# A half store and a weight fetch queued behind the first stacks of the fourth segment

## The chip, the core and the metric

The kernel runs on one core of a Trainium2 chip. The metric is device time of the whole program in microseconds (us), the median of several executions. Engine names are those of the profile: PE is the matmul engine (PEld its weight load), DVE the vector engine, ACT the scalar engine, POOL the GpSimd engine, and SP the sync engine, which here issues every DMA of the kernel, in one order, and computes nothing.

## What is computed

An adaLN block over 2048 tokens of width 1024: layernorm with a modulation, segmented attention with a compressive memory, a residual, a second modulated layernorm, and a token-mixing MLP. The attention is where the change lies. Cut to that:

```python
h = _layernorm(x) * (1 + ca) + sa
for s in range(4):                                  # segments of 512 tokens, 32 heads of 32
    qs, ks, vs = q[:, :, s], k[:, :, s], v[:, :, s] # h @ wq, h @ wk, h @ wv
    a_dot = softmax(qs @ ks.T * scale + mask) @ vs
    num, den = phi(qs) @ M, phi(qs) @ z + 1e-6
    o = g * num / den + (1.0 - g) * a_dot
    M, z = M + phi(ks).T @ vs, z + phi(ks).sum()
x = x + ga * (o @ wo)                               # then x + gb * mixer(layernorm(x) ...)
```

## The kernel before

Single-precision products are made of three reduced-precision ones: each operand is split into a high part (`hi`, an ACT copy, line 119) and the rest (`lo`, a DVE subtraction, line 122), so that a tile "has arrived" for PE in two steps.

**Order of the attention.** The heads are taken in 8 groups of four, the segments in two passes of two. An iteration `t` is one group in one segment of the pass: `t` = 0, 1 are group 0 in segments 0 and 1, `t` = 2, 3 are group 1 in the same two, `t` = 4, 5 group 2. What the title calls the fourth segment is the fourth iteration, `t` = 3. Each iteration has these steps, which the builder lays out over later and later slots, so that three iterations are in flight at a time:

- `project(t)`: matmuls of the group's k and v columns (`nps`, line 192; `kv_chunk`) and q columns (`qps`, line 200), then the split of k and q into a tile `sg`.
- `stack(t, h)` (lines 368 to 376): three DMAs of 128 KB, lines 374, 375 and 376, that lay the hi and lo parts of one head's q and k on top of each other in a tile `sk`. Line 374 takes the hi parts, 375 q's hi and k's lo, 376 q's lo and k's hi. There are two sets of four `sk` tiles, used by even and odd `t`.
- `maxima(t, h)` (line 478): three sorts of matmul, `sx`, `sy` and `sz`, out of the stack, and DVE's masked maxima of them (line 480); after two heads a transpose `nmps` (line 486) and the small stores of its result into `sk` (line 493).
- `scores(t, h)` (lines 515, 518 and 522, tiles `a`), exponentials on ACT into `p`, their split into `ph` (ACT, line 529) and the rest (POOL, line 531); `values(t, h)` (line 549, `pv`), whose normalisation on DVE is lines 552, 554 and 556.
- `memory(t)`: read-out `rd` (line 450) and update `up` (line 460).

Beside this run chores from a table `todo`, by slot number. Two matter here. `fetch_part` (line 150) loads half of a group's weights, 512 KB, into a tile tagged `raw` (three buffers), and `split_part` splits it later; `keep_w` (line 173) stores the split weights in DRAM for the second pass. `token_tile(tt)` (lines 252 to 272) prepares 128 tokens of the second pass's segments: it normalises the 512 KB tile `gaw`, and stores its hi part (`hix`, also a `raw` tile) and its lo part (in place in `gaw`) to DRAM, 512 KB each (line 271). Afterwards `load_gaw` (line 671) loads the next 128 tokens into the same `gaw`, which a DVE `BN_STATS` (line 127) reads first.

**Who sets the order.** A list scheduler orders each engine's instructions at build time by its own estimate of times. `tc.issue_after(x)` tells it to place what follows behind instruction `x`. On the chip each engine runs its list in that order, and so does SP with the DMAs.

Of the kernel before, what the change touches and what calls it, by code (L numbers as in the profile page):

```python
# [41 lines left out]
def attention_and_mlp(ctx, tc, x, wq, wkv, wo, beta, w1, b1, w2, b2, c, wm_a, wm_b, out):  # L42
    nc = tc.nc
    V, A, G, T, SY = nc.vector, nc.scalar, nc.gpsimd, nc.tensor, nc.sync
# [27 lines left out]
    def bank(tag, bufs, name):  # L72
        return psum.tile([P, 512], F32, tag=tag, bufs=bufs, name=name)
# [73 lines left out]

    def fetch_part(g, kind, part):
        r = a.tile([P, D], F32, tag="raw", bufs=3, name=f"raw{kind}{g}_{part}")
        SY.dma_start(r, (wkv if kind == "v" else wq)[g, :, 1024 * part:1024 * part + 1024])  # L150
        return r

    def split_part(g, kind, part, r):

        for i in range(2):
            w = aw.tile([P, 2, 512], F32R, tag="w", bufs=8, name=f"w{kind}0_{g}_{part}_{i}")
            split(w, r[:, 512 * i:512 * i + 512], A, V)
            W[0, g][kind, 2 * part + i] = w

    def load_part(g, pr, kind, part, res):  # L160

        if pr == 0:
            split_part(g, kind, part, fetch_part(g, kind, part))
            return
        for i in range(2):
            w = aw.tile([P, 2, 512], F32R, tag="w", bufs=8, name=f"w{kind}{pr}_{g}_{part}_{i}")
            SY.dma_start(w.bitcast(F32), wsp[g, 2 * part + i if kind == "v" else 4 + i])
            res[kind, 2 * part + i] = w

    def keep_w(g):  # L170
        for kind, n in (("v", 4), ("q", 2)):
            for i in range(n):
                SY.dma_start(wsp[g, i if kind == "v" else 4 + i], W[0, g][kind, i].bitcast(F32))
# [62 lines left out]
    def norm_x(pool, t):  # L236
        mv = ln_stats(pool, t, "a")
        V.tensor_scalar(mv[:, 3:4], mv[:, 0:1], -1.0, mv[:, 2:3], op0=ALU.mult, op1=ALU.mult)
        A.activation(t, t, AF.Identity, scale=mv[:, 2:3], bias=mv[:, 3:4])
# [12 lines left out]
    def token_tile(tt):  # L252

        r = gaw
        norm_x(a, r)
        for half in range(2):
            ps = bank("s2", 2, f"hpl{tt}_{half}")
            for i in range(4):
                ct = 4 * half + i
                T.transpose(ps[:, 128 * i:128 * i + 128], r[:, P * ct:P * ct + P], ident)  # L260
            for i in range(4):
                ct = 4 * half + i
                A.activation(r[:, P * ct:P * ct + P], ps[:, 128 * i:128 * i + 128], AF.Identity,
                             scale=saca[:, ct, 1:2], bias=saca[:, ct, 0:1])
        hi = a.tile([P, D], F32, tag="raw", bufs=3, name=f"hix{tt}")
        A.copy(hi.bitcast(F32R), r)
        for c in (slice(0, 512), slice(512, 1024)):
            G.tensor_tensor(r[:, c].bitcast(F32R), r[:, c], hi[:, c], op=ALU.subtract)
        i = tt % 4
        for part, t in enumerate((hi, r)):  # L270
            SY.dma_start(hT1[tt // 4 - 2, :, :, part, P * i:P * i + P].rearrange("k p n -> p k n"),
                         t.rearrange("p (k n) -> p k n", k=NK))

    right = tc.tile_pool(name="st2", bufs=1, side="right")
    s2p = right.__enter__()
# [90 lines left out]
    last_sk, last_nt = {}, {}  # L366
# [226 lines left out]
    todo = {}  # L593

    def plan(n, f, engines=""):
        todo.setdefault(n, []).append((f, engines))
# [21 lines left out]
    with tc.issue_after(normed_v.ins):  # L618
# [4 lines left out]
        with tc.issue_after(h_a.ins), tc.issue_after(h_v.ins):  # L623
            project(0, 2)
            project(0, 3)
    parts = (("v", 0), ("v", 1), ("q", 0))
    raw_1 = [fetch_part(1, *part) for part in parts]
    seg_chunks(1, 2, 8)
    project(1, 0)
# [33 lines left out]
    def later(n, fetch, m, f, engines):  # L663

        got = []
        plan(n, lambda: got.append(fetch()))
        plan(m, lambda: f(got[0]), engines)
# [5 lines left out]
    for i in range(8):  # L673
        later(6 * i, lambda i=i: load_gaw(i),
              6 * i + 3, lambda r, i=i: token_tile(8 + i), "V")
    for g in range(2, NG):
        n = 8 * g - 13
        plan(n, lambda g=g: W.__setitem__((0, g), {}))
        for kind, part, n0, n1 in (("v", 0, 0, 1), ("v", 1, 1, 3), ("q", 0, 2, 4)):
            later(n + n0, lambda g=g, kind=kind, part=part: fetch_part(g, kind, part),  # L680
                  n + n1, lambda r, g=g, kind=kind, part=part: split_part(g, kind, part, r), "A")
        plan(n + 4, lambda g=g: keep_w(g))
# [8 lines left out]
    for n in range(-LEADS, 4 * NI + VL):  # L691
# [5 lines left out]
        if 0 <= m + 4 < 4 * NI:  # L697
            t = (m + 4) // 4
# [448 lines left out]
```

## Time and profile before

| | us |
|---|---|
| median of 3 runs | 2222.85 (2221.31 to 2225.35) |
| the profiled execution | 2224.45 |
| its span, first to last instruction | 2222.7 |
| what lies around the span | 1.75 |
| mean granted PE clock | 0.997 |
| PE, DVE, ACT and POOL busy | 98%, 75%, 51%, 33% of the span |

In a timeline each row has a start, a length, the engine, the line of the kernel, the operation, out<-in by the program's names without numbers, and in brackets the idle time of the engine ahead of it and what ended it. "issue" there means that the profile shows nothing that the engine waited for; a DMA's landing can stand behind it. A row with a count merges equal instructions. Rows marked SPq are DMAs at their issue on SP. In a table of stretches the number in brackets counts instructions; PEclk is the granted clock, and the DMA share can be over 1 because packets overlap.

### The profile page before, as it was taken

What the parts mean: (1) busy time and instruction counts of PE and PEld (TensorE: products, weight loads), DVE (VectorE), ACT (ScalarE), POOL (GpSimd) and SP (SyncE); (2) the same over time, 40 slices, a digit from 0 to 9 for tenths busy, and PEclk for the clock granted to TensorE, in tenths of its full rate; (3) what the DMA queues carried; (4) which work ended last, traced back from release to release, by engine and by line L of the source; (5) the groups of instructions that cost most, each with busy time, mean ns of one, the idle gap of its engine ahead of it and who ended that gap; (6) DMA issues with size and microseconds to landing.
All of it is one profiled execution on the core that took longest, in us unless ns stands there. A gap on an engine that the chain in (4) does not pass through costs nothing.

```text
span 2222.7 us, 38130 instructions
## 1 busy us (share of the span) xinstructions
PE 2184.5 (98%) x13786; PEld 1881.3 (85%) x13786; DVE 1673.2 (75%) x3762; ACT 1132.7 (51%) x2050; POOL 723.6 (33%) x831
## 2 busy tenths in 40 slices
PE   8999999999999999999999999999999999999999
PEld 5988998889999999888888888888888888888887
DVE  7677777767777677664858766888888887869687
ACT  5476777755666666654636533533334242424232
POOL 2165766656767677553002200033330000000000
PEclk9999999999999999999999999999999999999999
DMA  7656665587566665664754686655556541414134
GB/s 287 193 172 195 183 185 160 169 297 246 167 195 203 199 206 176 192 227 133 232 204 185 227 318 255 246 225 207 214 203 222 199 153 60 142 57 147 57 124 152
DMA packets 175184, 423.05 MB, mean 190 GB/s; under 512 B 17524, under 2 KB 71828, under 8 KB 166036
## 3 DMA queue, kind: packets, MB, share of 16 engines
q1 hardware_dynamic: 174996, 420.61, 57.4%
q8 instruction: 110, 1.80, 0.3%
q14 instruction: 78, 0.64, 0.1%
HBM read 244.62 MB, written 125.06 MB: 166 GB/s over the span
## 4 chain that ended last, share of the span: by engine, by line
PE 82%; DVE 6%; DMA 5%; ACT 3%; issue 1%; POOL 1%; SPq 1%; DVEq 0%; ACTq 0%
PE mx L927 47%; PE nps L192 10%; PE qps L200 7%; PE po L797 6%; PE pv L549 3%; DMA otr<-oT 1%; PE a L515 1%; DMA sk<-sg 1%; PE sz L478 1%; PE sx L478 1%; POOL p L531 1%; PE a L522 1%; PE sy L478 1%; PE a L518 1%; PE up L460 1%
## 5 line engine op out<-in xcount | busy, mean ns | idle before, releaser
L927 PE MATMUL mx<-bU,sp 128*128 128x512 f32 x2352 | 534.7, 389 | 1.0 <-DVE ac L934 0.9
L927 PEld LDWEIGHTS mx<-bU,sp 128*128 128x128 f32 x2352 | 441.1, 188 | 94.1 <-issue 1.3
L119 ACT CAST sp<-wr 128x384 fp32r<-128x384 f32 (+2 forms) x408 | 217.2, 545 | 433.0 <-PE mx L927 354.8
L192 PE MATMUL nps<-wv,h 128*128 128x256 f32 x3072 | 430.9, 283 | 1.1 <-DVE h L122 0.7
L927 PE MATMUL mx<-bA,sp 128*128 128x512 f32 x1764 | 430.5, 389 | 0.0
L531 POOL TENSOR_TENSOR p<-p,ph 128x640 f16<-128x640 f32 x256 | 377.7, 1476 | 121.7 <-ACT ph L529 116.8
L192 PEld LDWEIGHTS nps<-wv,h 128*128 128x128 f32 x3072 | 402.7, 190 | 8.8 <-DVE h L122 1.8
L927 PEld LDWEIGHTS mx<-bA,sp 128*128 128x128 f32 x1764 | 331.2, 188 | 68.7
L122 DVE TENSOR_TENSOR sp<-wr,sp 128x384 fp32r<-128x384 f32 (+2 forms) x408 | 259.1, 646 | 28.9 <-ACT sp L119 28.7
L934 DVE TENSOR_TENSOR ac<-mx,ac 128x512 f32<-128x512 f32 x280 | 189.4, 685 | 85.1 <-PE mx L927 84.5
L200 PE MATMUL qps<-h,wq 128*128 128x512 f32 x768 | 196.4, 399 | 0.0
L529 ACT CAST ph<-p 128x1280 f16<-128x1280 f32 x128 | 161.1, 1258 | 49.7 <-POOL p L527 49.2
L797 PE MATMUL po<-wo,ots 128*128 128x512 f32 x768 | 179.7, 391 | 1.4 <-ACT ots L119 1.4
L527 POOL TENSOR_SCALAR_AFFINE_SELECT p<-p 128x256 f32<-128x256 f32 x256 | 135.5, 535 | 119.9 <-ACT p L524 70.4
L797 PEld LDWEIGHTS po<-wo,ots 128*128 128x128 f32 x768 | 143.4, 188 | 31.2 <-ACT ots L119 1.8
L927 PE MATMUL mx<-bB,sp 128*128 128x512 f32 x588 | 164.0, 389 | 0.0
L200 PEld LDWEIGHTS qps<-h,wq 128*128 128x128 f32 x768 | 140.5, 189 | 27.1
L927 PEld LDWEIGHTS mx<-bB,sp 128*128 128x128 f32 x588 | 110.4, 188 | 22.9
L934 DVE TENSOR_TENSOR cc<-mx,cc 128x512 f32<-128x512 f32 x140 | 94.9, 684 | 41.7 <-PE mx L927 41.6
L480 DVE CUSTOM_DVE_ANT_0 sz<-sz,mask 128x512 f32<-128x512 f32 x128 | 89.2, 697 | 47.8 <-PE sz L478 46.9
L480 DVE CUSTOM_DVE_ANT_0 sx<-sx,mask 128x128 f32<-128x128 f32 (+1 forms) x256 | 93.3, 365 | 35.2 <-PE sx L478 31.5
L516 ACT ACTIVATE p<-a,shift 128x512 f32<-128x512 f32 x128 | 88.0, 688 | 43.6 <-PE a L515 39.6
(207 smaller groups left out, 3193.9 us busy)
## 6 DMA issues: line engine op xcount, KB each, us to landing
sk<-sg SPq DMA_DIRECT2D x384, 128.0 KB
wr<-in_w_dram SPq DMA_DIRECT2D x28, 1024.0 KB
wr<-in_w_dram SPq DMA_DIRECT2D x32, 768.0 KB
bstu<-ucd SPq DMA_DIRECT2D x28, 768.0 KB
wsp<-wv SPq DMA_DIRECT2D x32, 512.0 KB
rawm<-in_wm_b_dram SPq DMA_DIRECT2D x32, 512.0 KB
wv<-wsp SPq DMA_DIRECT2D x32, 512.0 KB
pcd<-cc SPq DMA_DIRECT2D x14, 1024.0 KB
```

The costliest lines, as they stand in the source:

```text
L119: last_hi[0] = A.copy(hi, src)
L122: return lo_eng.tensor_tensor(lo, src, hi.bitcast(F32), op=ALU.subtract)
L192: T.matmul(ps[:, aa], h[:, j, 128 * tt:128 * tt + 128], wt[:, i, o:o + 256], start=(n == 0), stop=(n >= 6 * NK - 2), skip_group_check=True)
L200: T.matmul(ps, wt[:, i, o:o + 128], h[:, j], start=(k + n == 0), stop=(3 * k + n == 3 * NK - 1))
L480: marks[4 * t + h - LEADS, "V"] = V.tensor_tensor_reduce(o, o, mask[:, 384 - 128 * i:], 1.0, -3.0e38, op0=ALU.add, op1=ALU.max, accum_out= ...
L516: A.activation(p32[:, 0:512], b0, AF.Exp, scale=SCALE, bias=shift)
L527: G.affine_select(w, w, pattern=[[0, 2], [1, 128]], compare_op=ALU.is_ge, fill=0.0, base=0, channel_multiplier=-1)
L529: marks[n, "A"] = A.copy(hi, p32)
L531: marks[n, "G"] = G.tensor_tensor(lo[:, c], p32[:, c], hi[:, c], op=ALU.subtract)
L797: T.matmul(ps, os_[:, i, P * ct:P * ct + P], wop[ct, nh][:, j], start=(n == 0), stop=(n == 3 * NK - 1))
L927: T.matmul(ps, ops[q][:, i, P * k:P * k + P], b[:, j], start=(m == 0 and first), stop=(m == 3 * nk - 1), skip_group_check=True)
L934: V.tensor_tensor(d, ps, d, op=ALU.add)
```

## The change

`token_tile` stores its hi part as before. For the first token tile (`tt` = 8) the store of the lo part goes into slot 6 of the `todo` table, at its head, and is placed behind the last DMA of `stack(3, 0)`. The fetch of the third group's q weights (`g` = 2) moves from slot offset 2 to 3, and is placed behind the same DMA. Nothing else is edited; no byte is added or taken away.

```diff
     def fetch_part(g, kind, part):
         r = a.tile([P, D], F32, tag="raw", bufs=3, name=f"raw{kind}{g}_{part}")
-        SY.dma_start(r, (wkv if kind == "v" else wq)[g, :, 1024 * part:1024 * part + 1024])
+        with ExitStack() as s:
+            if g == 2 and kind == "q":
+                s.enter_context(tc.issue_after(last_sk[3, 0].ins))
+            SY.dma_start(r, (wkv if kind == "v" else wq)[g, :, 1024 * part:1024 * part + 1024])
         return r
...
         i = tt % 4
-        for part, t in enumerate((hi, r)):
+
+        def keep(part, t):
             SY.dma_start(hT1[tt // 4 - 2, :, :, part, P * i:P * i + P].rearrange("k p n -> p k n"),
                          t.rearrange("p (k n) -> p k n", k=NK))
+
+        def keep_behind_stack():
+            with tc.issue_after(last_sk[3, 0].ins):
+                keep(1, r)
+
+        keep(0, hi)
+        if tt == 8:
+            todo[6].insert(0, (keep_behind_stack, ""))
+        else:
+            keep(1, r)
...
         for kind, part, n0, n1 in (("v", 0, 0, 1), ("v", 1, 1, 3), ("q", 0, 2, 4)):
+            if g == 2 and kind == "q":
+                n0 = 3
             later(n + n0, lambda g=g, kind=kind, part=part: fetch_part(g, kind, part),
```

The built programs differ on three engines, all within one stretch: SP, PE and DVE. The lists of ACT and POOL are the same. In the lists below lines of the changed kernel are 14 higher from line 282 on (376 is 390, 478 is 492, 549 is 563), those of the fetch and of `kv_chunk` 3 higher (150 is 153, 192 is 195); names carry their buffer numbers.

SP before, from the hi store of token tile 8 on. `sk1_0` and `sk1_1` are the stacks of heads 0 and 1 of `t` = 3, `hT1` is the DRAM home of the token tiles.

```order
L271 DMA hT1_66<-hix8_1355 128x8x128
L374 DMA sk1_0_501<-sg3_1667 32x2x512
L375 DMA sk1_0_501<-sg3_1667 32x2x512
L271 DMA hT1_66<-gaw_77 128x8x128
L150 DMA rawq2_0_1601<-in_wq_dram 128x1024
L376 DMA sk1_0_501<-sg3_1667 32x1024
L374 DMA sk1_1_502<-sg3_1667 32x2x512
L375 DMA sk1_1_502<-sg3_1667 32x2x512
L376 DMA sk1_1_502<-sg3_1667 32x1024
L671 DMA gaw_77<-in_x_dram 128x1024
L173 DMA wsp_65<-wv0_2_0_0_1480 128x1024
L173 DMA wsp_65<-wv0_2_0_1_1483 128x1024
```

SP in the changed kernel, the same piece.

```order
L275 DMA hT1_66<-hix8_1355 128x8x128
L388 DMA sk1_0_501<-sg3_1664 32x2x512
L389 DMA sk1_0_501<-sg3_1664 32x2x512
L390 DMA sk1_0_501<-sg3_1664 32x1024
L388 DMA sk1_1_502<-sg3_1664 32x2x512
L389 DMA sk1_1_502<-sg3_1664 32x2x512
L390 DMA sk1_1_502<-sg3_1664 32x1024
L275 DMA hT1_66<-gaw_77 128x8x128
L153 DMA rawq2_0_1726<-in_wq_dram 128x1024
L176 DMA wsp_65<-wv0_2_0_0_1479 128x1024
L685 DMA gaw_77<-in_x_dram 128x1024
L176 DMA wsp_65<-wv0_2_0_1_1482 128x1024
```

The lo store and the q weights moved behind both stacks, and the load of the next token tile moved behind the first of the two weight stores.

PE before, in the same stretch: scores of `t` = 1, head 2, ten pairs of weight load and matmul of `pv1_0`, projections of `t` = 4, and then the first maxima of `t` = 3.

```order
L518 MATMUL a1_1_2_1608<-sk1_2_503 128x384
L549 LDWEIGHTS ph1_0_1364
L549 MATMUL pv1_0_1641<-vp1_860,ph1_0_1364 128x97
...
L192 MATMUL nps4_0_1895<-wv0_2_0_0_1480,h0_0_254 128x256 x4
L478 MATMUL sx_3_0_1964<-sk1_0_501 128x128
L478 MATMUL sx_3_0_1964<-sk1_0_501 128x256
L478 MATMUL sy_3_0_1969<-sk1_0_501 128x384
L192 MATMUL nps4_0_1895<-wv0_2_0_0_1480,h0_0_254 128x256 x2
```

PE in the changed kernel.

```order
L532 MATMUL a1_1_2_1605<-sk1_2_503 128x384
L492 MATMUL sx_3_0_1964<-sk1_0_501 128x128
L492 MATMUL sx_3_0_1964<-sk1_0_501 128x256
L492 MATMUL sy_3_0_1969<-sk1_0_501 128x384
L563 LDWEIGHTS ph1_0_1363
L563 MATMUL pv1_0_1638<-vp1_860,ph1_0_1363 128x97
...
L195 MATMUL nps4_0_1895<-wv0_2_0_0_1479,h0_0_254 128x256 x6
```

The three maxima moved ahead of the ten `pv1_0` pairs and of the first projections, so the six projections with that tile now stand together; the first four of the six read the weights' hi part, the last two the lo part.

DVE before, behind the last step of splitting the values of `t` = 3 (`vp3`): the normalisation of `pv1_0` and the maxima of `t` = 3, head 0.

```order
L438 TENSOR_TENSOR vp3_1786<-r1_3_1787,vp3_1786 128x16x32
L552 RECIPROCAL pv1_0_1641<-pv1_0_1641 128x4
L480 ISA sx_3_0_1964,mx3_0_1963<-sx_3_0_1964,mask_93 128x128
L480 ISA mx3_0_1963 128x1
L554 TENSOR_REDUCE red1_0_1663<-pv1_0_1641 128x128
L480 ISA sy_3_0_1969,mx3_0_1963<-sy_3_0_1969,mask_93 128x384
```

DVE in the changed kernel.

```order
L452 TENSOR_TENSOR vp3_1786<-r1_3_1787,vp3_1786 128x16x32
L566 RECIPROCAL pv1_0_1638<-pv1_0_1638 128x4
L568 TENSOR_REDUCE red1_0_1660<-pv1_0_1638 128x128
L494 ISA sx_3_0_1964,mx3_0_1963<-sx_3_0_1964,mask_93 128x128
L494 ISA mx3_0_1963 128x1
L494 ISA sy_3_0_1969,mx3_0_1963<-sy_3_0_1969,mask_93 128x384
```

The reduction of `pv1_0` moved ahead of the first maximum; a few more rows up to about 30 us later trade places in the same way.

## The prediction, made before the changed kernel had run

> **What bounds the kernel now.** I read the page first: its shares, and its chain of work that ended last.
>
> ```profile
> PE 2184.5 (98%) x13786; PEld 1881.3 (85%) x13786; DVE 1673.2 (75%) x3762; ACT 1132.7 (51%) x2050; POOL 723.6 (33%) x831
> ...
> PE 82%; DVE 6%; DMA 5%; ACT 3%; issue 1%; POOL 1%; SPq 1%; DVEq 0%; ACTq 0%
> ```
>
> PE is busy for 2184.5 of 2222.7 us. All its waiting is 38 us, and a change of order can win only what it finds of that at its own place, and the slow clock that follows. So I went to that place with PE's timeline.
>
> ```profile
> 130.87 0.42 PE L518 MATMUL a<-sk 98*128 98x384 f32 x1
> 131.58 0.61 PE L549 MATMUL pv<-vp,ph 128*128 128x97 bf16 x10 [0.29 <-ACT ph L529]
> 132.10 0.74 PE L192 MATMUL nps<-wv,h 128*128 128x256 f32 x4
> 135.16 0.47 PE L478 MATMUL sx<-sk 96*128 96x128 f32 x2 [2.33 <-issue]
> ...
> 135.65 1.08 PE L192 MATMUL nps<-wv,h 128*128 128x256 f32 x6
> ...
> 140.91 0.36 PE L549 MATMUL pv<-vp,p 128*128 128x65 bf16 x6
> 141.10 0.95 PE L192 MATMUL nps<-wv,h 128*128 128x256 f32 x6
> 141.89 0.27 PE L486 MATMUL nmps<-ident,mx 128*8 128x128 f32 x1
> ...
> 143.59 0.46 PE L478 MATMUL sz<-sk 96*128 96x512 f32 x1
> ```
>
> The reader is to see 2.33 us of idle ahead of `sx`, which by the order is the first maxima matmul of t = 3, with the releaser "issue". It reads the stack of head 0, so I looked at SP's issues.
>
> ```profile
> 126.78 0.69 SPq L374 DMA_DIRECT2D sk<-sg  x1
> 127.57 0.65 SPq L375 DMA_DIRECT2D sk<-sg  x1
> 128.30 0.54 SPq L271 DMA_DIRECT2D hT<-gaw  x1
> 128.93 0.64 SPq L150 DMA_DIRECT2D rawq<-in_wq_dram  x1
> 129.67 1.09 SPq L376 DMA_DIRECT2D sk<-sg  x1
> ...
> 132.83 0.53 SPq L671 DMA_DIRECT2D gaw<-in_x_dram  x1
> 133.60 2.13 SPq L173 DMA_DIRECT2D wsp<-wv  x2
> ```
>
> The stack's third part is issued at 129.67, behind a store and a load of 512 KB each, and `sx` starts 135.16 - 129.67 = 5.49 us later. How long does such a part take with nothing large just ahead of it? Later another first maxima matmul waits for its stack, and there the profile names the DMA:
>
> ```profile
> 317.11 0.56 SPq L376 DMA_DIRECT2D sk<-sg  x1
> ...
> 319.53 0.47 PE L478 MATMUL sx<-sk 96*128 96x128 f32 x2 [0.74 <-DMA sk<-sg]
> ```
>
> That is 2.42 us. The 3.07 us between them are what 1 MB takes at 340 GB/s, and the DMA engines are full at our place, as a table of stretches shows (its last three columns are granted clock, DMA share and GB/s):
>
> ```profile
> 132.71:136.12 3.41, 1.08 (x10) 0.99 (x8) 3.38 (x4) 3.41 (x6) 2.74 (x3) 1.00 1.07 278
> 136.12:139.54 3.42, 3.42 (x21) 3.33 (x20) 3.42 (x3) 0.82 (x2) 3.34 (x3) 0.50 0.97 375
> ...
> 140.00:142.00 2.00, 2.00 (x24) 1.95 (x22) 0.20 (x2) 0.58 (x1) 0.41 (x1) 1.00 0.40 96
> ...
> 477.46:480.87 3.41, 1.87 (x19) 1.70 (x17) 1.61 (x7) 0.07 (x1) 2.80 (x2) 1.00 0.23 61
> 480.87:484.28 3.41, 3.41 (x40) 3.06 (x38) 2.31 (x7) 2.36 (x6) 0.55 (x3) 1.00 0.69 130
> 491.11:494.52 3.41, 1.56 (x16) 1.05 (x16) 2.69 (x6) 1.55 (x4) 3.13 (x2) 1.00 0.96 359
> 494.52:501.35 6.83, 6.25 (x31) 5.99 (x32) 3.10 (x11) 4.05 (x7) 4.81 (x7) 0.50 0.92 335
> ```
>
> The wait has a second price. The stretch with 1.08 us of PE work in 3.41 is followed by 3.42 us at half the clock, which do 1.71 us less work. The same follows 1.56 us of work, and does not follow 1.87. So the brink is a stretch of 3.41 us with between 1.54 and 1.85 us of idle.
>
> Last DVE, which holds the other end:
>
> ```profile
> 132.08 3.29 DVE L122 TENSOR_TENSOR wv<-rawv,wv 128x512 fp32r<-128x512 f32 x2 [0.61 <-ACT wv L119]
> ...
> 138.11 1.90 DVE L438 TENSOR_TENSOR vp<-r,vp 128x512 bf16<-128x512 f32 x1
> 141.30 0.19 DVE L552 RECIPROCAL pv<-pv 128x4 f32<-128x4 f32 x1 [1.29 <-PE pv L549]
> 142.20 0.30 DVE L480 CUSTOM_DVE_ANT_0 sx<-sx,mask 128x128 f32<-128x128 f32 x1 [0.70 <-PE nmps L486]
> ...
> 144.16 0.68 DVE L480 CUSTOM_DVE_ANT_0 sz<-sz,mask 128x512 f32<-128x512 f32 x1
> ...
> 144.77 1.27 DVE L127 BATCH_NORM_STATS2 st<-gaw 128x6 f32<-128x512 f32 x2
> ```
>
> DVE is through with `vp` at 138.11 + 1.90 = 140.01, and then waits for a late PE twice, 1.29 and 0.70 us.
>
> **The change, part by part.** No instruction and no byte is added or removed.
>
> *The stack's third part* now follows the second directly, so it is issued at about 128.30, where the moved store went out. When it lands there, no row of before shows. Bounds: 2.42 us after issue as in the quiet place, 130.72, and 5.49 as now, 133.79. I take about 131, near the first, since the megabyte that makes up the difference stands behind it now; the loads and the store ahead of both stay.
>
> *PE* reaches `sx` behind the scores of 130.87, at about 131.1. `sy` behind it waits for DVE's last maxima, done at 132.08 - 0.61 = 131.47, and ends at about 131.7. The ten `pv` and the first four `nps` take 132.84 - 131.58 = 1.26 us, to 132.95. Then come the two `nps` that read the weights' lo part. That part is ready at 133.60: the first `wsp` store, which also reads it, goes out then. So PE waits 0.65 us, and starts them at 133.60, where before they started at 135.65: **2.05 us earlier**. From there to `nmps` it was 141.89 - 135.65 = 6.24 us, of which 1.71 went to the half clock, so 4.53 of work. The stretch around 133 now has some 0.8 us of idle, under the brink, so I count full clock, and 0.2 us for the second lo part, which DVE ends at 132.08 + 3.29 = 135.37. `nmps` is then at 138.3, the last `pv` ends 0.6 ahead of it, at 137.7.
>
> *DVE.* Both come before 140.01, so DVE's two waits go: 1.29 + 0.70 = **1.99 us**. Can DVE be through with `vp` earlier than 140.01? I find nothing for it: what it works on from 132.08 on comes from ACT, and ACT's first wait for PE in these microseconds comes after it fed `vp`:
>
> ```profile
> 137.42 0.63 ACT L437 CAST vp<-r 128x512 bf16<-128x512 f32 x1 [1.10 <-DVE r L436]
> 140.14 0.58 ACT L524 ACTIVATE p<-a,shift 128x384 f32<-128x384 f32 x1 [2.09 <-PE a L522]
> ```
>
> So what is late next is DVE, and PE now waits for it: `sz` needs the bank that DVE's maxima of `sx` read. PE gets there 143.59 - 141.89 = 1.70 us behind `nmps`, at 140.0, and DVE lets it go 1.99 us earlier than now, at 141.6. Some 1.6 us of PE's win are waited off again. From here on DVE and PE are both 1.99 us ahead of before. The trade of places on DVE (the reduction of `pv` ahead of a maximum) costs nothing by itself: the same rows, with neither input late.
>
> *What stands behind now.* The q weights' fetch leaves SP some 2.6 us later than 128.93; they are first read here:
>
> ```profile
> 150.72 1.14 ACT L119 CAST wq<-rawq 128x512 fp32r<-128x512 f32 x2
> ...
> 155.31 1.14 PE L460 MATMUL up<-v,pk 128*128 128x132 f32 x8 [0.98 <-DVE pv L552]
> ```
>
> Cover of 19 us, cost nothing. The lo store leaves at about 128.30 + 4 x 0.65 = 130.9. The next load of `gaw` must wait until that store has read the tile (now at most 132.83 - 128.30 = 4.5 us after its issue), so until 135.4 at the latest, and it stands behind the first `wsp` store too. Its data is wanted by `BN_STATS`, at 144.77 - 1.99 = 142.8, so it has 7.4 us; the DMA share falls to 0.40 in 140 to 142, so the queue is then empty. Cost nothing; if it came later than 142.8, DVE would stand still with all that is queued behind, one us for each us. While SP waits for `gaw`, the second `wsp` store and the stack of head 2 wait behind it. That stack waits for scores anyway:
>
> ```profile
> SPq L374 <- PE a L522: 10.1, 4, 4.3
> ```
>
> *Sum.* 1.99 us. Against the profiled execution: 2224.45 - 1.99 = 2222.46. That execution is 1.6 us above the median of the runs shown; against the median, 2222.85 - 1.99 = **2220.9**. Does it last? Later waits, such as the 0.98 us ahead of `up` above, are of PE for DVE, and both are shifted alike.
>
> *A rule against this reading of the clock.* The trace's stretch with 1.08 us of work, so 2.33 of idle, is followed by half the clock. The Trainium skill, "TensorE: Matmul & The Clock Gate", section "HAM oscillation — how this bites in real kernels", puts the abstract rule as no idle gaps over about 3.4 us. By that rule the 2.33 us would not have cost the clock, the half clock would stay at 136.12 in the changed kernel, `nmps` would come at about 139.9, still before DVE is free, and the sum would stay 1.99; only the first rival below would shrink, to 2.05. The rows of 1.08 and 1.56 us of work speak against it, so I go by the rows.
>
> **Rivals.**
>
> - *DVE does not hold PE back* (its order or what it waits for shifts so that PE keeps all): 2.05 + 1.71 = 3.76 us, 2219.1. For it: PE has 82% of the chain. Against it: DVE's rows from 132.08 to 140.01 have no gap that PE makes.
> - *The half clock only moves.* PE's new idle of 1.6 us at 140.0 is at the brink. If it falls over it, 1.71 us of PE work are lost in a dense stretch, less the 0.98 us that PE waits ahead of `up` anyway: 1.99 - 0.73 to 1.99 - 1.71, about 0.8 us won, 2222.0.
> - *The change does not do what it says*: the queue is full already when the third part goes out, and it takes its 5.49 us all the same. Then `sx` starts at 133.79, the two `nps` follow 0.49 + 1.26 = 1.75 us later, at 135.54, and 0.1 us is won: 2222.7. For it: the DMA share about 1 all through the stretch.
> - *Slower, since `sx` now stands ahead of `pv` and `nps`*, which before filled 1.26 us of the wait. The point from which it decides: 133.90 + 1.75 = 135.65, so a landing later than 133.90, 5.60 us after issue. With a landing as late as now, 135.16, the two `nps` start at 136.91, 1.26 us later than before: 2224.1. Against it: a megabyte no longer stands ahead.
>
> **How the numbers follow.** The forecast gets 0.45, the first rival 0.08, the moved half clock 0.20, no effect 0.17, slower 0.10. The predicted time is the forecast's, 2220.9; its own range is 1.5 us to either side, which is about how the three runs of before scatter. The range reaches from 2218.5, below the first rival's 2219.1 by part of that scatter, to 2224.2, just over the slower one's. About what a measurement of this kernel can tell from no change is 0.2%, 4.45 us, so below 2218.4 or above 2227.3. No case reaches these by itself; with the scatter I give faster 0.08, slower 0.05, and same 0.87.
>
> **What would show it.** Right: SP issues the third part directly behind the second; `sx` starts near 131 with no idle over 0.5 us ahead; the idle moves to the two `nps` at 133.6, released by DVE `wv`, and to `sz`, released by DVE; DVE's reciprocal follows `vp` without a gap; clock 1.00 from 136 to 140. Wrong: a DMA or "issue" wait over 1 us ahead of `sx` (the landing), a wait of `BN_STATS` for `gaw`, a half clock around 143, or DVE through with `vp` at another time than 140.

## The result, and the profile after

| | median us | runs | ratio to before, 95% interval |
|---|---|---|---|
| before | 2223.18 (2218.42 to 2229.40) | 22 | |
| changed | 2220.34 (2216.53 to 2225.07) | 22 | 0.9986 (0.998 to 0.9993) |
| changed, second comparison | 2218.36 (before: 2222.89) | 12 | 0.9986 (0.9975 to 0.9997) |
| changed, third comparison | 2219.27 (before: 2222.60) | 11 | 0.9988 (0.9978 to 0.9998) |
| before against itself | 2223.04 (before: 2222.60) | 11 | 1.0 (0.9991 to 1.0009) |

The changed kernel is faster by 0.0014 x 2223 = 3.1 us, with 1.6 to 4.4 us in the interval. The forecast was 2220.9, a gain of 1.99, and "within 0.2%". The profiled execution has a span of 2218.6 us (2222.7 before). Two slow executions further down are in none of the times: one of the split on GpSimd (4838 us), and the profiled one of "fetch alone" (10248 us), whose rows are used only up to 519 us, where its granted clock falls.

TensorE, VectorE, ScalarE, GpSimd and SyncE are the profile's PE, DVE, ACT, POOL and SP.

TensorE's timeline of the changed kernel, around the moved transfers and at a mark 200 us later, the transposes `kps`:

```profile
130.87 0.42 PE L532 MATMUL a<-sk 98*128 98x384 f32 x1
132.30 0.47 PE L492 MATMUL sx<-sk 96*128 96x128 f32 x2 [1.01 <-DMA sk<-sg]
132.61 0.34 PE L492 MATMUL sy<-sk 96*128 96x384 f32 x1
132.79 0.84 PE L563 MATMUL pv<-vp,ph 128*128 128x97 bf16 x10
133.41 3.48 PE L195 MATMUL nps<-wv,h 128*128 128x256 f32 x16
136.73 0.30 PE L563 MATMUL pv<-vp,p 128*128 128x65 bf16 x4
...
139.15 0.36 PE L563 MATMUL pv<-vp,p 128*128 128x65 bf16 x6
...
140.13 0.27 PE L500 MATMUL nmps<-ident,mx 128*8 128x128 f32 x1
...
141.72 0.39 PE L492 MATMUL sz<-sk 96*128 96x512 f32 x1
...
334.38 0.66 PE L419 MATMUL kps<-ident,k 128*128 128x128 f32 x4 [0.99 <-ACT v L413]
```

The wait ahead of `sx` fell from 2.33 to 1.01 us, `nmps` moved from 141.89 to 140.13, and `sz`, for which the forecast had 1.6 us of waiting, starts without any. The same mark in the kernel before:

```profile
336.13 0.66 PE L405 MATMUL kps<-ident,k 128*128 128x128 f32 x4 [1.00 <-ACT v L399]
```

SyncE of the changed kernel: the third part goes out at 128.30, the store of `gaw` behind both stacks, and the next load of `gaw` (L685) waits from 133.9 to 135.23.

```profile
128.30 0.56 SPq L390 DMA_DIRECT2D sk<-sg  x1
...
130.94 0.53 SPq L275 DMA_DIRECT2D hT<-gaw  x1
131.52 0.69 SPq L153 DMA_DIRECT2D rawq<-in_wq_dram  x1
133.59 0.33 SPq L176 DMA_DIRECT2D wsp<-wv  x1
135.23 0.33 SPq L685 DMA_DIRECT2D gaw<-in_x_dram  x1
```

VectorE of the changed kernel:

```profile
138.11 1.90 DVE L452 TENSOR_TENSOR vp<-r,vp 128x512 bf16<-128x512 f32 x1
139.93 0.18 DVE L566 RECIPROCAL pv<-pv 128x4 f32<-128x4 f32 x1
140.14 0.56 DVE L568 TENSOR_REDUCE red<-pv 128x128 f32<-128x384 f32 x1
140.62 0.29 DVE L494 CUSTOM_DVE_ANT_0 sx<-sx,mask 128x128 f32<-128x128 f32 x1
...
142.15 0.71 DVE L494 CUSTOM_DVE_ANT_0 sz<-sz,mask 128x512 f32<-128x512 f32 x1
...
142.79 1.27 DVE L127 BATCH_NORM_STATS2 st<-gaw 128x6 f32<-128x512 f32 x2
```

`vp` starts at 138.11 in both profiles. The reciprocal now follows without a gap; `sz` came 2.01 us earlier than before (144.16) and `BN_STATS` 1.98 us earlier (144.77). At the mark 334.38 the lead is 336.13 - 334.38 = 1.75 us. ScalarE shows the same lead where it waited for TensorE, 1.89 us (before 140.14, with 2.09 of waiting):

```profile
138.25 0.58 ACT L538 ACTIVATE p<-a,shift 128x384 f32<-128x384 f32 x1 [0.20 <-PE a L536]
```

The stretches of 3.41 us on which the granted clock changes, in the changed kernel (granted clock, DMA share and GB/s are the last three columns):

```profile
129.59:133.00 3.41, 2.17 (x15) 1.51 (x16) 2.80 (x9) 3.41 (x7) 2.07 (x3) 1.00 1.06 257
133.01:136.42 3.41, 3.41 (x23) 3.41 (x21) 3.38 (x4) 3.30 (x6) 2.74 (x3) 0.50 1.07 293
136.42:139.83 3.41, 3.41 (x37) 3.33 (x37) 3.41 (x3) 1.22 (x2) 3.41 (x4) 1.00 1.00 361
```

The half clock is still there, one stretch earlier, and explains the 3.48 us of the `nps` at 133.41.

### The profile page after: what moved, and what is told of

It is laid out like the page before. It is cut to its first block, busy times and chain, and to the rows that moved or that the text cites. A ratio compares the mean times of both kernels' runs of the same rounds, so it can differ in the third digit from the quotient of the medians.

```text
span 2218.6 us, 38129 instructions
## 1 busy us (share of the span) xinstructions
PE 2183.0 (98%) x13786; PEld 1879.1 (85%) x13786; DVE 1674.1 (75%) x3762; ACT 1132.9 (51%) x2050; POOL 720.0 (32%) x831
## 4 chain that ended last, share of the span: by engine, by line
PE 83%; DVE 7%; DMA 4%; ACT 2%; issue 1%; POOL 1%; SPq 1%; DVEq 0%; ACTq 0%
PE mx L943 48%; PE nps L195 10%; PE po L813 7%; PE qps L203 6%; PE pv L563 3%; DMA rawm<-in_wm_b_dram 2%; PE a L529 1%; PE sz L492 1%; PE sx L492 1%; POOL p L545 1%; DMA sk<-sg 1%; PE a L536 1%; DVE wv L122 1%; PE srow L308 1%; PE a L532 1%
```

## The experiments

Runs of one kernel scatter by some 5 us to either side, and two profiles of the kernel before have spans of 2222.7 and 2219.5. So the mechanism is read from marks inside one profile. In all kernels of this table VectorE's `vp` starts 9.9 us behind the `sz` that stands at 128.20 in the profile of before, so marks are counted from its start, in us: the reciprocal, VectorE's maximum of `sz`, and the mark `kps`.

| kernel | wait ahead of `sx` | reciprocal | `sz` | `kps` | ratio, 95% interval |
|---|---|---|---|---|---|
| before | 2.33 | 3.19 | 6.05 | 198.02 | |
| before, second profile | 2.56 | 3.42 | 6.28 | 198.32 | 1.0 (0.9991 to 1.0009) |
| changed | 1.01 | 1.82 | 4.04 | 196.27 | 0.9986 (0.998 to 0.9993) |
| changed, second profile | none | 1.82 | 4.03 | 196.16 | 0.9986 (0.9975 to 0.9997) |
| changed, third profile | 0.80 | 1.82 | 4.03 | 196.05 | 0.9988 (0.9978 to 0.9998) |
| store alone | 3.15 | 4.48 | 7.08 | 199.29 | 1.0008 (0.9996 to 1.002) |
| fetch alone | 2.01 | 2.43 | 5.04 | 197.23 | 1.0003 (0.9994 to 1.0012) |
| first half of the store too | none | 1.83 | 4.03 | 198.74 | 0.9991 (0.9981 to 1.0) |
| maxima later, DMAs as before | none | 1.82 | 4.03 | 196.20 | 0.9994 (0.9983 to 1.0005) |
| three transfers ahead | 1.01 | 1.82 | 4.30 | 196.51 | 0.998 (0.9969 to 0.9992) |

**The theory:** VectorE sets the pace here. It is done with `vp` 1.8 us after it starts, and each us that TensorE's `pv` and `nmps` come later is lost, while nothing is gained where they come sooner. TensorE takes its work in order, so what counts is how long it stands at `sx` with these still behind. **Rivals:** TensorE sets the pace, and each us that it waits counts; or what counts is only how many bytes stand ahead of the stack's third part.

### One half of the change at a time

Store alone, as a difference from the changed kernel:

```diff
-            if g == 2 and kind == "q":
-                s.enter_context(tc.issue_after(last_sk[3, 0].ins))
...
-            if g == 2 and kind == "q":
-                n0 = 3
```

> The lo store goes behind both stacks, the q weights' fetch stays ahead of the third part of stack 0. Marks: the start of BN_STATS on gaw was 144.77 us before and 142.79 with the whole change; first maxima of t = 3 135.16 and 132.30. My account (PE parked at those maxima makes DVE wait): 512 KB ahead in place of 1 MB, the third part is issued near 128.95 and lands near 133.8, so the maxima start near 133.8, the lo projections near 135.5, BN_STATS between 142.9 and 144.6 by whether the half clock hits the same stretch; 0.2 to 1.9 us faster than before. Rival (the gain goes with the bytes ahead of the stack): half of the gain, 1.5 us. Rival (PE's own idle and clock are the gain, DVE holds nothing): 1.4 us of wait less, so 1.4 us faster.

Measured: 2225.08 (before: 2221.49). SyncE, TensorE and VectorE of this kernel:

```profile
127.75 0.65 SPq L387 DMA_DIRECT2D sk<-sg  x1
129.94 0.34 SPq L151 DMA_DIRECT2D rawq<-in_wq_dram  x1
130.37 0.56 SPq L388 DMA_DIRECT2D sk<-sg  x1
```

```profile
134.62 0.77 PE L490 MATMUL sx<-sk 96*128 96x128 f32 x2 [3.15 <-DMA sk<-sg]
```

```profile
142.76 0.19 DVE L564 RECIPROCAL pv<-pv 128x4 f32<-128x4 f32 x1 [2.59 <-PE pv L561]
```

The fetch now stands directly behind the second part, and SyncE stands at it from 128.4 to 129.94 with the third part behind. What it waits for is the store of the hi part out of its `raw` buffer (from SyncE's waits of 124 to 136 us):

```profile
SPq L151 <- DMA hT<-hix: 1.5, 1, 1.5
```

`sx` starts at 134.62, which is earlier than in the kernel before (135.16), and yet VectorE's wait for `pv` doubles, to 2.59 us: `pv` and the projections, which before filled the time ahead of `sx`, now stand behind it.

Two things in this profile are not shown to come from the edit. The loads of the v weights, ahead of all that is edited, went out 0.6 us later than in both profiles of the kernel before (122.49 - 0.18 = 122.31, against 121.67), and with them may go the wait at the fetch: "maxima later" below, with the DMA order of before, has one of 1.8 us, and neither profile of before has any. And the clock is at half for 6.83 us, from 133.14 on, against 3.41 before: behind `sx` 5.35 us in place of 3.41, so about 1.0 us more of TensorE's work lost, an estimate from these times that is nearly all of the loss in the table. That half of the change is worse than none is therefore not shown.

Fetch alone, as a difference from the changed kernel:

```diff
-        if tt == 8:
-            todo[6].insert(0, (keep_behind_stack, ""))
-        else:
-            keep(1, r)
+        keep(1, r)
```

> The q weights' fetch goes behind the stack, the lo store stays ahead of its third part. As with the store alone: third part issued near 128.9, maxima near 133.8, BN_STATS 142.9 to 144.6, 0.2 to 1.9 us faster than before by my account, 1.5 by the rival of the bytes ahead, 1.4 by the rival of PE's own idle. If the two parts of the change do different things, one of these two runs has all of the gain (BN_STATS at 142.8) and the other none (144.8).

Measured: 2222.99 (before: 2221.49).

```profile
133.90 0.47 PE L489 MATMUL sx<-sk 96*128 96x128 f32 x2 [2.01 <-DMA sk<-sg]
```

```profile
141.13 0.19 DVE L563 RECIPROCAL pv<-pv 128x4 f32<-128x4 f32 x1 [0.55 <-PE pv L560]
```

The store alone stands 1.1 us later at `kps` than the mean of the two profiles of before (198.17), the fetch alone 0.9 earlier, both together 2.0 earlier (196.16, the mean of three). These kernels and the changed one have the same order on TensorE and VectorE, and differ only in SyncE's queue. The totals of the two halves show neither, since both intervals hold 1. With a wait of 3.15 us at `sx` the reciprocal stands at 4.48, with 2.01 at 2.43, and with 1.01, 0.80 or none at 1.82: up to about 1 us the wait costs nothing, as the theory has it and the first rival has not.

### The first half of the store behind the stacks too

```diff
         def keep_behind_stack():
             with tc.issue_after(last_sk[3, 0].ins):
+                keep(0, hi)
                 keep(1, r)
-        keep(0, hi)
         if tt == 8:
             todo[6].insert(0, (keep_behind_stack, ""))
         else:
+            keep(0, hi)
             keep(1, r)
```

> The hi store of the token tile goes behind the stacks as well, so that only the two weight loads stand ahead. The third part is issued near 128.3 and lands near 130.9. My account: the maxima start near 131.1 with no wait over 0.3 us, the 1.01 us wait of the changed kernel and perhaps its half clock go, but BN_STATS stays at 142.8 (within 0.3), since DVE is free at 140.0 in any case: as fast as the changed kernel, 2 to 3 us below before. Rival (PE's own idle and clock are the gain): a further 1.0 us and up to 1.7 us from the clock, 4 to 5.5 us below before, BN_STATS near 141.

Measured: 2221.26 (before: 2221.49; 0.9991, 0.9981 to 1.0). The wait at `sx` is gone, and nothing is gained up to `sz` (4.03). Behind it the next load of `gaw` has become late:

```profile
137.29 0.78 SPq L686 DMA_DIRECT2D gaw<-in_x_dram  x1
```

```profile
145.55 1.29 DVE L127 BATCH_NORM_STATS2 st<-gaw 128x6 f32<-128x512 f32 x2 [1.82 <-DMA gaw<-in_x_dram]
```

At `kps` this kernel stands at 198.74, 0.6 us later than before. So the load of `gaw`, which the prediction costed at nothing up to a landing at 142.8, has a cover that a second 512 KB store uses up. (A half clock of 3.41 us from 148.14 on may share in the 0.6 us.) The ratio does not show this loss; it leaves open what the kernel wins back behind 465 us.

### The order on TensorE without the change

"Maxima later" is the kernel before with its order of DMAs, and the maxima matmuls of the first stack (`sx`, `sy`; some of the recorded expectations call them scores) held until TensorE has done the first 24 projections of `t` = 4, those with the first half of the v weights. `kv_mark` is the last of these 24:

```diff
...
-        at(maxima, n + LEADS)
+        with ExitStack() as s:
+            if n + LEADS == 12:
+                s.enter_context(tc.issue_after(kv_mark[0].ins))
+            at(maxima, n + LEADS)
```

> The DMA order is that of before; the first maxima of t = 3 are placed on PE behind the first half's projections of four chunks, so that PE does other work while the stack is on its way. My account: the stack lands as late as before, near 135.1, PE comes to the maxima near 136.4 and does not wait, the lo projections start near 133.6, BN_STATS at 142.8: 2 to 3 us faster than before, the whole gain with no DMA moved. Rival (the stack must arrive earlier): the time of before, within 0.5 us, BN_STATS at 144.8.

Measured: 2220.84 (before: 2221.49; 0.9994, 0.9983 to 1.0005). The total stands nearer to the rival's 0.5 us than to the 2 to 3 us expected, and its interval holds both, so it decides nothing. The marks do: `kps` stands 2.0 us below the mean of before.

```profile
134.25 1.65 PE L194 MATMUL nps<-wv,h 128*128 128x256 f32 x12 [0.80 <-DVE wv L122]
...
137.10 0.23 PE L482 MATMUL sx<-sk 96*128 96x128 f32 x1
```

The third part went out at 131.76 here, and this profile stands 0.64 us later than that of before: 131.12, where it was 129.67. So the stack was later still, and it cost nothing.

"Three transfers ahead" is the kernel before with one more store of 512 KB, to a place that nobody reads, ahead of the third part:

```diff
...
+        if tt == 8:
+            extra[0] = SY.dma_start(spare, r)
...
-        last_sk[t, h] = SY.dma_start(skf[64:96], src[:, 1:3])
+        with ExitStack() as s:
+            if (t, h) == (3, 0):
+                s.enter_context(tc.issue_after(extra[0].ins))
+            last_sk[t, h] = SY.dma_start(skf[64:96], src[:, 1:3])
```

The program's order follows from this: the maxima of the first stack move behind the same 24 projections here too.

> The kernel before, with a third store of 512 KB (the low part of token tile 8, to a place that nobody reads) ahead of the first stack's third part: more bytes ahead of that part than before, not fewer. The scores of this stack then stand further back on TensorE, behind all first-half projections. Account (what counts is whether TensorE is parked at `sx` while its sums for VectorE are due): the gain of the change without the change, RECIPROCAL with no gap behind `vp`, `sz` 4.0 us after `vp` begins, 2220.5 to 2222. Rival (what counts is how many bytes stand ahead of the third part): slower than the kernel before by 1 to 2 us, 2224.5, and VectorE waits over 1.3 us for `pv`.

Measured: 2218.11 (before: 2222.89; 0.998, 0.9969 to 0.9992). SyncE, TensorE and VectorE:

```profile
128.85 0.64 SPq L277 DMA_DIRECT2D spare<-gaw  x1
130.47 0.35 SPq L151 DMA_DIRECT2D rawq<-in_wq_dram  x1
130.91 1.21 SPq L384 DMA_DIRECT2D sk<-sg  x1
```

```profile
137.79 0.50 PE L486 MATMUL sx<-sk 96*128 96x128 f32 x2 [1.01 <-DMA sk<-sg]
```

```profile
138.08 1.90 DVE L446 TENSOR_TENSOR vp<-r,vp 128x512 bf16<-128x512 f32 x1
139.90 0.18 DVE L560 RECIPROCAL pv<-pv 128x4 f32<-128x4 f32 x1
```

A stack that is used 6.88 us after its issue, after a wait for it, later than in any other kernel here, costs nothing where `sx` stands behind the projections. So the bytes ahead do not decide by themselves. At `kps` both kernels win 1.7 to 2.0 us of the mean before, without any transfer moved out of the way. The total of this one fell by 0.2%, 4.4 us, which is more than its mark shows and more than was expected; where the rest comes from is not shown.

### Maxima behind the projections in the changed kernel

The changed kernel with the same kind of hold, at the fourth projection of `t` = 4 instead of the 24th.

> The changed kernel, with TensorE's scores of the first stack of token tile 3 put behind the first four of the second-half projections, as where the stack comes late. TensorE's wait of 1.01 us at `sx` should go. Account (VectorE sets the pace): nothing is gained over the changed kernel, 2220.3 us give or take 0.7, and `sz` on VectorE again 4.0 us after `vp` begins. Rival (TensorE sets the pace, and each us that it waits counts): 1.0 us less than the changed kernel, 2219.3, and `sz` about 3 us after `vp` begins.

Measured: 2226.42 (before: 2222.89; 1.0019, 1.0008 to 1.003), 6 us or more above what either theory said. The wait at `sx` went, and up to 144 us the marks stand within 0.3 us of the changed kernel's, counted from the `sz` ahead of the change: VectorE's `sz` comes 0.2 us sooner, not the 1.0 of the rival. One row there is new:

```profile
143.28 1.28 DVE L127 BATCH_NORM_STATS2 st<-gaw 128x6 f32<-128x512 f32 x2 [0.34 <-DMA gaw<-in_x_dram]
```

This load of `gaw` went out at 135.68 and was used 7.60 us later. In the changed kernel it went out at 135.23 and `BN_STATS` started 7.56 us later.

Further back the hold changed the program's order: compared record by record, some 4,400 of the 13,786 matmuls in the two traces stand elsewhere, where the kernels before and changed differ in 10. At `kps`, whose own place may have changed, this kernel is already 5.4 us behind the changed one. So its total is one of another order, and tells nothing of the theory.

### Taking work from VectorE

The low parts of the third group's first v weights on GpSimd:

```diff
-            split(w, r[:, 512 * i:512 * i + 512], A, V)
+            split(w, r[:, 512 * i:512 * i + 512], A, G if (g, kind, part) == (2, "v", 0) else V)
```

> The changed kernel, with the low parts of the first half of the third group's v weights subtracted on GpSimd in place of VectorE, which frees 3.3 us of VectorE at 132 to 135 us. Account (VectorE sets the pace at 130 to 144 us): the marks behind this stretch come earlier by 1 to 3 us (the full 3.3 only where the sums of TensorE and the load of `gaw` keep up), about 2218.5 us. Rival (TensorE or the transfers set it): no gain, 2220.3, or slower where GpSimd's longer subtraction holds the split weights back.

Measured: 2220.35 (before: 2222.89; 0.9987, 0.9974 to 1.0). VectorE and TensorE:

```profile
133.38 0.69 DVE L433 SCALAR_TENSOR_TENSOR pq<-qps,rq 128x512 f32<-128x512 f32 x1 [1.66 <-ACT rq L431]
...
140.59 0.70 DVE L494 CUSTOM_DVE_ANT_0 sz<-sz,mask 128x512 f32<-128x512 f32 x1
```

```profile
142.47 1.21 PE L195 MATMUL nps<-wv,h 128*128 128x256 f32 x8 [1.23 <-ACT wv L119]
...
332.61 0.66 PE L419 MATMUL kps<-ident,k 128*128 128x128 f32 x4 [0.99 <-ACT v L413]
```

`sz` comes at 140.59 in place of 142.15, and `kps` at 332.61 in place of 334.38, though the profile starts 0.24 us later (VectorE's `sz` ahead of the change at 128.44 against 128.20): 2.0 us are won of the 3.3 taken off, and then TensorE waits for ScalarE. So VectorE did set the pace up to there. The total, for which some 2218.5 was expected, does not show the further 2.0 us. A second comparison of this kernel:

> The kernel with the third group's first v split on GpSimd once more, on another chip. In its first profile VectorE's work stood 3.7 us earlier than before from 145 to 465 us, 2.0 us more than in the changed kernel, and the measured gain was 2.9 us with an interval from 0 to 5.8. If the 2.0 us reach the end, about 2219.0 and a ratio near 0.998; if they are lost in the waits behind 470 us, 2220.5 and 0.9988, as for the change alone.

Measured: 2219.17 (before: 2223.56; 0.9981, 0.9969 to 0.9993). Neither comparison parts it from the changed kernel. The same split for all groups from the third on:

> The changed kernel with the first v split of every group from the third on (six of them) on GpSimd. It moves instructions in all segments behind 145 us too. If VectorE sets the pace at each of these splits, 1 to 2 us less per group where TensorE has idle time there, some 2216 us; rival: TensorE is busy over 97% in nearly all stretches behind 145 us, nothing further is gained there, and the new order costs some us, 2221 to 2226, as with the maxima held back.

Measured: 2231.99 (before: 2223.56; 1.0031, 1.0018 to 1.0044). The rival was right that nothing further is gained, but the kernel is 7 us slower than before, beyond the 2226 that it allowed. Against the split of one group some 4,500 of the 13,786 matmuls stand elsewhere; whether that order or GpSimd's own work costs the time is not parted.

### The same two kernels again

> The changed kernel again, beside the next three on one chip. Account (VectorE sets the pace here once TensorE's sums come by the time that it is done with its subtraction): about 2220.3 us, 3 us below the kernel before, RECIPROCAL behind the subtraction `vp` with no gap, and the product `sz` on VectorE 4.04 us after `vp` begins (6.05 before). If the 3 us were scatter of the first chip, the ratio comes out at 1.000 here.

Measured: 2218.36 (before: 2222.89; 0.9986, 0.9975 to 0.9997). TensorE in this second profile of the changed kernel:

```profile
134.10 1.68 PE L195 MATMUL nps<-wv,h 128*128 128x256 f32 x12 [0.67 <-DVE wv L122]
...
139.22 0.27 PE L500 MATMUL nmps<-ident,mx 128*8 128x128 f32 x1
...
142.02 0.50 PE L492 MATMUL sz<-sk 96*128 96x512 f32 x1 [1.05 <-DVE mx L494]
```

Here the clock stays whole, `nmps` comes 1.39 us sooner against `vp` (139.22 - 138.59 = 0.63 after its start, 2.02 in the first profile), and TensorE waits it off ahead of `sz`. VectorE's marks are the same to 0.01 us. It is the same kernel with and without the half clock, and a second time nothing is gained where TensorE comes sooner.

The stack also landed earlier here. What goes with that stands ten microseconds earlier. SyncE's rows of the first profile, and below them of this one, which stands 0.48 us later:

```profile
117.67 1.68 SPq L389 DMA_DIRECT2D sk<-sg  x1
122.77 0.91 SPq L153 DMA_DIRECT2D rawv<-in_wkv_dram  x2
```

```profile
118.14 0.60 SPq L389 DMA_DIRECT2D sk<-sg  x1
122.15 0.91 SPq L153 DMA_DIRECT2D rawv<-in_wkv_dram  x2
```

In the first profile one issue took 1.68 us in place of 0.60, and the loads of the v weights, 512 KB each, went out 1.1 us later and closer to the stack. The same holds for the third profile (1.47 us; the loads 0.9 us later). No row shows why the issue took longer; it is not the change, since the three profiles are of one kernel. That the later loads delay the stack fits all three, but no run sets them apart.

> The kernel before, once more, for a second profile. In its first one the clock is at half for 6.83 us from 494.5 us on, in five profiles of kernels that gain at 140 us for 3.41 us or not at all, and their marks move ahead by another 1.3 us between 495 and 515 us. If the longer half clock belongs to the kernel before, this profile shows 6.83 us again, and about 1.3 us of the 3.1 measured come from there. If it is chance, 3.41 us here, and the marks at 515 us stand 1.3 us earlier than in the first profile. The time: a ratio of 1.000, whose interval shows what such a comparison can tell.

Measured: 2223.04 (before: 2222.60; 1.0, 0.9991 to 1.0009). The half clock of 6.83 us at 494.5 does not come again (there is one of 3.41 at 467 in its place), so this kernel does not always have it. The store alone has one as long, from 494.96 on; what decides it stays open.

> The changed kernel for a third profile and a third comparison: `sz` on VectorE 4.04 us after `vp` begins, the mark at the k transposes (335 us) 1.8 us earlier than before, 3.41 us of half clock near 494 if that belongs to the kernel, and a ratio of 0.9986 as twice measured; 0.9992 if only the 1.8 us of the stretch at 140 us reach the end.

Measured: 2219.27 (before: 2222.60; 0.9988, 0.9978 to 0.9998); `kps` stands 2.1 us below the mean of before. No half clock stands near 494 us in this profile, so the one of 3.41 us there does not belong to the changed kernel either.

## Why the prediction was right

- **DVE's two waits, 1.99 us**: right, 2.01 at `sz` and 1.98 at `BN_STATS`. At `kps` three profiles of the changed kernel and two of before differ by 198.17 - 196.16 = 2.0 us, so it lasts that far. The maxima held back without the change and the work taken from VectorE show the cause.
- **TensorE's path to `nmps`, 138.3**: right in the second profile, which stands 0.48 us later. There TensorE waited 0.67 us for `wv` (0.65 said), went on at 134.10 - 0.48 = 133.62 (133.60 said), and came to `nmps` at 138.74. In the first profile it was wrong, and in part luck hid it: the stack landed late, the clock was at half, the first projection that reads the lo part started at 134.41, and `nmps` came at 140.13, behind the 140.01 that it had to precede. The prediction took the trade of places on VectorE as free; here it was what kept the second wait away, since the reduction of `pv` ran first. In the old order the maximum of `sx` would have waited about 0.3 us, an estimate from the end of the reciprocal at 140.11 and of `nmps` at 140.40.
- **The third part lands near 131**: right in the second profile, where `sx` starts without a wait at 131.60 - 0.48 = 131.12, so at most 2.82 us after the issue, near the 2.42 of the quiet place. In the other two it was 1.1 to 1.3 us too early: 4.00 and 3.8 us (130.58 to 134.38) from issue to use. The step that failed there is "the loads and the store ahead of both stay": the loads went out some 1 us later. Where they went out alike, as in the second profile and in the kernel before, the megabyte made at least 5.49 - 2.82 = 2.67 us, near the 3.07 said. The DMA engines stayed full without it (a share of 1.06 from 129.59 to 133.00). The wait of 1.01 us in the first profile is also just what the prediction named as a sign of being wrong. The error cost nothing, since `nmps` ended at 140.40, 0.2 us ahead of VectorE's maximum of `sx` at 140.62. That is all the slack there was in this profile.
- **Full clock, under the brink of 1.54 to 1.85 us of idle**: wrong. 2.17 us of work in 3.41, so 1.24 of idle, was followed by half the clock. So was 1.03 us of idle in the kernel "maxima behind the projections" (263.72 to 267.13). In the second profile of the kernel before, 1.84 us of work (1.57 idle) was not:

```profile
132.84:136.25 3.41, 1.06 (x8) 1.10 (x9) 3.38 (x4) 3.27 (x6) 2.76 (x2) 1.00 1.08 264
136.26:139.66 3.40, 3.40 (x21) 3.31 (x20) 3.40 (x3) 0.63 (x1) 2.99 (x3) 0.50 0.98 377
818.92:822.33 3.41, 1.84 (x17) 1.64 (x15) 3.07 (x10) 0.37 (x1) 3.33 (x2) 1.00 0.56 132
822.34:825.75 3.41, 2.92 (x33) 2.66 (x33) 1.86 (x9) 1.81 (x4) 1.43 (x4) 1.00 0.78 296
```

  Idle time in such a stretch does not decide it alone. The rival "the half clock only moves" came about in one of three profiles, to 133.01 and not to 143, where VectorE was busy anyway and it cost nothing. The rule of the Trainium skill that was weighed ("TensorE: Matmul & The Clock Gate", section "HAM oscillation — how this bites in real kernels": no idle gaps over about 3.4 us) is contradicted here as well, by a half clock behind a longest gap of 1.01 us.
- **PE waits 1.6 us ahead of `sz`**: none in the first profile, 1.05 and 1.08 in the other two. Where the clock was whole the wait was there, of the forecast's kind and 0.5 us shorter.
- **The fetch and the load of `gaw` cost nothing**: right. The load went out at 135.23 (forecast 135.4 at the latest), and `BN_STATS` did not wait. But there was hardly any cover in the "7.4 us": with the maxima behind the projections the same load took 7.60 us, and `BN_STATS` waited. With the split on GpSimd it took at most 6.04 (135.31 to 141.35).
- **The rival "slower, since `sx` stands ahead"**: the store alone met its condition. With that profile 0.17 us later, its `sx` at 134.62 is past the 133.90 from which it decides. The first of its `nps` starts at 136.33, and the fifth, the first to read the lo part, at 137.33: 2.71 us behind `sx`, at half clock, where 1.75 was said for full clock. So the longer path is shown, and what it costs at full clock is not.
- **The size**: the three comparisons give 2.7 to 3.1 us, the marks 2.0. All three intervals hold 2.0 (a ratio of 0.9991), so the rest is not shown to exist; no place for it could be found, since behind 465 us profiles of one kernel differ by 3 us.

## What to carry to other kernels

Where an engine takes its work in order, a late DMA is priced by what stands behind the waiting instruction and by when the next engine wants it. Find the engine that those results feed, and when it is free; earlier than that, a better landing gains nothing. Before two profiles are compared, look whether what stands ahead of the edit ran alike: here one slow issue ten microseconds earlier went with a landing more than 1 us later. Any move through a scheduler may also reorder thousands of instructions elsewhere: count them before a total is put down to the edit.

## What was not expected of the hardware

The same transfer of 128 KB, with no large one directly ahead, took 4.00, at most 2.82 and 3.8 us from issue to use in three profiles of one kernel; in the two late ones an issue ten microseconds earlier had taken 1.68 and 1.47 us in place of 0.60. The half clock came behind less idle time than elsewhere left it whole. And the 1.7 us of TensorE's work lost to it in the first profile did not move VectorE's marks at all, since VectorE was not waiting for TensorE.
